# Retention followed by a four-expert MLP on one core: a batch's remainder on another queue, and the second token tile begun by halves between a later batch's units

## Chip, cores and metric

The kernel runs on one core of a Trainium2 chip. The metric is device time in microseconds for one execution, the median over the runs shown. The engines are named as in the profile: PE (TensorE matmuls), PEld (its weight loads), DVE (VectorE), ACT (ScalarE), POOL (GpSimd), SP (SyncE, which only issues DMAs here). POOL's DMAs go through a software queue, those of SP and ACT through hardware queues.

## The reference, cut to what matters

```python
# q, k, v: (B=8, H=8, S=576, D=64); moe_w1: (E=4, 512, F=1024); moe_w2: (4, 1024, 512)
scores = q @ k.T / 8                                  # per batch and head
Dmat = where(i >= j, gamma[h] ** (i - j), 0)          # decay with distance
x = ((scores * Dmat) @ v), heads side by side         # (4608, 512)
p = domain_probs / (sum over experts + 1e-9)          # (4608, 4)
out = sum over e of p[:, e] * (relu(x @ w1[e]) @ w2[e])
```

## The kernel before

**Two stages that overlap.** The tokens, 8 batches of 576, are cut into 9 tiles of 512 tokens (`t` = 0 to 8). A batch does not fill a tile evenly: tile 0 holds the first 512 tokens of batch 0, tile 1 the last 64 of batch 0 (its *remainder*) and 448 of batch 1, and so on. The retention stage writes the transposed tile `xt_of(t)` (bf16, features on the partitions); the MLP of tile `t` reads it. All work is put into one program order by hand; each engine runs its own instructions in that order and waits on semaphores for the others.

**Retention by units.** The first 512 tokens of batches 0 and 1 are done in four `Unit`s each: a unit is 256 tokens (`hf`) of four heads (`g`). A unit casts its raw k, q and v to bf16 with decay factors (`cast`, L526), transposes q and k either on PE (`trans_pe`, L534) or by DMA from SP (`trans_dma`, L547), multiplies scores and masks them on DVE (`scores`, L556), adds up the state `sbd` from k and v (`kv`, L587), and multiplies values (`values_own`, `values_carried`, L616 to L656), which ACT copies into `xt` (L649, L653). Batches 2 to 7 use a larger form, `Duo`. The remainder of each batch is a `Rem` (L320): loads (`load_rem`, L79: five DMAs, 384 KB in pieces of 256 bytes), casts, two DMA transposes on SP (L339), scores (L345), values (L351, L353).

**The MLP of a tile.** Up projections: 16 groups (`up_group`, L360), four per expert, each of 16 matmuls of 512 columns, followed on DVE by relu times the mixing weight `pB[t, e]` (L369) into `h`. Tile 0's first two groups are replaced by two `UpHalf`s (L374), each for 256 of the 512 tokens and four feature chunks, so that PE can begin before all tokens are there. Down projections: tile 0's first 256 tokens are done by plain products (`Plain`, L392, `po`), one block of eight matmuls per expert and half; its last 256 tokens, and all later tiles, by seven products per 256 tokens (`Down.product`, L448), which need sums of weights (`w_sum`, L410, tiles `t2w`, `t3w`, `t4w` and, in place, `wx[0]`) and sums of `h` (`sums`, L436), all on DVE.

**Loads.** POOL loads the weights, converted to bf16 on the way: `load_w1(e)` (L99, 1024 KB in the tile) and `load_w2(e)` (L102), and between them the mixing weights `pB` (`load_p`, L235). Line by line, L716 to L753 give POOL's order: pB of expert 1, w1 of expert 1, small tables, pB and w1 of experts 2 and 3, w2 of experts 0 and 1, batch 0's remainder, w2 of experts 2 and 3, then the raw tensors of batch 1's first two units (`load_v(0)`, `load_v(1)`). The raw tensors of batch 1's other two units are loaded from SP into the same buffers, after the first two have been cast (`v_cast`, L766).

**Slots.** What is neither an up group nor a product is hung on numbered slots: `add(i, f)` puts `f` into slot `i`, and `run(slots, n)` emits a slot's work after the n-th step of the tile. For tile 0, slots 0 to 15 follow the up groups (expert 0's first two are passed over, since the halves did them), 16 to 23 the plain products, 24 to 30 the seven products in the order 1, 5, 2, 3, 6, 7, 4 (L797 to L814). Batch 0's remainder stands at slots 17 (casts on DVE, transposes on SP), 20 (scores) and 21 (values); batch 1's units are at slots 23 to 29; `w_sum` at 20 to 27. From tile 1 on a slot table of 30 steps per tile is filled in the same way (L822 to L871).

**Buffers.** Accumulators in PSUM come from one ring of four (`ring_tile`); the accumulator `pd` of the seven products holds one of them until product 4 is read. `pB` and two of batch 1's bf16 buffers share a pool of four.

Of the kernel before, what the change touches and what calls it, by code (L numbers as in the profile page):

```python
# [23 lines left out]
def kernel(  # L24
# [10 lines left out]
    nc = tc.nc  # L35
    B, H, S, D = q.shape
    N, E = moe_domain_probs.shape
    _, Dm, F = moe_w1.shape
# [7 lines left out]
    NDC = Dm // 128  # L46
# [19 lines left out]
    def ring_tile(name, shape, dt=FP32):  # L66
        return ring.tile(shape, dt, tag="ring", name=name)
# [5 lines left out]
    def load_pair(t, b, p, eng=nc.sync):  # L73
        for n, src in srcs:
            for j in range(2):
                eng.dma_start(out=t[n][:, :, j, :],
                              in_=src[b, 2 * p + j, 0:SM, :].rearrange("(c p) d -> p c d", p=C))

    def load_rem(b, eng=nc.sync):  # L79
        for j in range(2):  # L80
            for n, src in (("k", k), ("v", v)):
                eng.dma_start(out=rawr[n][64 * j:64 * j + 64, :, j, :],
                                  in_=src[b, j:H:2, SM:S, :].rearrange("g t d -> t g d"))
        eng.dma_start(out=rawr["q"][0:R, :, :, :].rearrange("t g j d -> t (g j) d"),
                          in_=q[b, :, SM:S, :].rearrange("h t d -> t h d"))
# [3 lines left out]
    raw1 = {n: const.tile([128, NC, 2, D], FP32, name=f"raw1_{n}") for n, _ in srcs}  # L89
# [9 lines left out]
    def load_w1(e, f=slice(0, F)):  # L99
        return nc.gpsimd.dma_start(out=w1_sb[e][:, :, f], in_=moe_w1[e][:, f].rearrange("(dc p) f -> p dc f", p=128))  # L100

    def load_w2(e, lo=0, hi=NFC):  # L102
        c = (e % 2) * NFC
        return nc.gpsimd.dma_start(
            out=wx[e // 2][:, c + lo:c + hi, :, :].rearrange("p a b c -> p a (b c)"),
            in_=moe_w2[e][lo * 128:hi * 128, :].rearrange("(fc p) d -> p fc d", p=128))
# [67 lines left out]
    def later_tables():  # L174
        nc.gpsimd.memset(tri, 1.0)
        nc.gpsimd.affine_select(out=tri, in_=tri, compare_op=mybir.AluOpType.is_ge, fill=0.0,
                                base=0, channel_multiplier=-1, pattern=[[1, C]])
        nc.gpsimd.tensor_copy(trir[0:R], tri[0:R, 0:R])
        nc.gpsimd.tensor_copy(trir[R:2 * R], tri[R:2 * R, R:2 * R])
        nc.gpsimd.iota(pos_j[:, 0:NC], pattern=[[C, NC]], base=0, channel_multiplier=1,  # L180
                       allow_small_or_imprecise_dtypes=True)
        for j in range(2):
            nc.gpsimd.iota(pos_j[64 * j:64 * j + 64, NC:NC + 1], pattern=[[0, 1]], base=SM, channel_multiplier=1,
                           allow_small_or_imprecise_dtypes=True)
        for n in "kqv":
            nc.gpsimd.memset(rawr[n], 0.0)
# [46 lines left out]
    pB = {}  # L233

    def load_p(t, e, eng):  # L235
        pB[t, e] = ppool.tile([128, NT], FP32, tag="pB", name="pB")
        eng.dma_start(out=pB[t, e], in_=pd[e:e + 1, t * NT:(t + 1) * NT].to_broadcast([128, NT]))  # L237
# [4 lines left out]
    def xt_of(t):  # L242
        if t not in xt:
            xt[t] = xpool.tile([128, NDC, NT], BF16, tag="xt", name="xt")
        return xt[t]


    class Duo:
        def __init__(self, b, d):
            self.b, self.d = b, d  # L250
            self.ps = slice(2 * d, 2 * d + 2)
            self.qT, self.kT, self.sT = {}, {}, {}
# [107 lines left out]
    def up_group(h, t, e, i):  # L360
        ph = ring_tile("ph", [128, 2, NT])
        x = xt_of(t)
        for f in range(2):
            fc = 2 * i + f
            for dc in range(NDC):
                nc.tensor.matmul(ph[:, f, :], lhsT=w1_sb[e][:, dc, fc * 128:(fc + 1) * 128],  # L366
                                 rhs=x[:, dc, :], start=(dc == 0), stop=(dc == NDC - 1))
        fk = e * NFC + 2 * i
        nc.vector.scalar_tensor_tensor(h[:, fk:fk + 2, :], ph, 0.0,  # L369
                                       pB[t, e][:, :].unsqueeze(1).to_broadcast([128, 2, NT]), op0=MAX, op1=MULT)  # L370
        if i == NFC // 2 - 1 and 0 < t < n_nt - 1:
            load_p(t + 1, e, nc.gpsimd)

    class UpHalf:  # L374


        def __init__(self, half):
            self.c = slice(256 * half, 256 * half + 256)
            self.ph = ring_tile("ph", [128, 4, 256])

        def matmuls(self, i):
            for fc in range(2 * i, 2 * i + 2):
                for dc in range(NDC):
                    nc.tensor.matmul(self.ph[:, fc, :], lhsT=w1_sb[0][:, dc, fc * 128:(fc + 1) * 128],
                                     rhs=xt_of(0)[:, dc, self.c], start=(dc == 0), stop=(dc == NDC - 1))

        def relu(self, h):
            nc.vector.scalar_tensor_tensor(h[:, 0:4, self.c], self.ph, 0.0,
                                           pB[0, 0][:, self.c].unsqueeze(1).to_broadcast([128, 4, 256]),
                                           op0=MAX, op1=MULT)  # L390

    class Plain:  # L392
# [291 lines left out]
    for u in range(NU):  # L684
        if u + 2 < NU:
            cast_unit(u + 2)
        if u == NU - 1:
            part = UpHalf(0)
# [21 lines left out]
    h = hp.tile([128, E * NFC, NT], BF16, name="h")  # L710
    part.relu(h)
    part = UpHalf(1)
    part.matmuls(0)
    part.matmuls(1)
    part.relu(h)
    load_p(0, 1, nc.gpsimd)  # L716
    load_w1(1)
    later_tables()
    load_p(0, 2, nc.gpsimd)
    load_w1(2)  # L720
# [2 lines left out]
    load_w2(0, 0, NFC // 2)  # L723
    load_w2(0, NFC // 2, NFC)
    load_w2(1)
    load_rem(0, nc.gpsimd)
    load_w2(2)
    load_w2(3)
    down1 = Down(h, 0, 1)
# [25 lines left out]
    def run(slots, i):  # L755
        for f in slots.get(i, []):
            f()

    slots = {}
    add = lambda i, f: slots.setdefault(i, []).append(f)  # L760
    add(4, later_decays)
    rem0 = Rem(0)
    for at, f in ((17, lambda: rem0.cast(nc.vector)), (17, rem0.trans_dma), (20, rem0.scores), (21, rem0.values)):
        add(at, f)

    def v_cast(u):  # L766
        vs[u].cast("k", nc.gpsimd)
        vs[u].cast("q", nc.vector)
        vs[u].cast("v", nc.scalar if u < 0 else nc.gpsimd)
        if u > 1:  # L770
            vs[u].trans_dma()
        else:
            load_v(u + 2, nc.sync)

    def v_head(u):
        vs[u].scores()
        vs[u].kv()

    for u, (c, tr, sc, o) in enumerate(((23, 24, 25, 26), (24, 25, 26, 27), (25, 0, 27, 28), (26, 0, 28, 29))):
        add(c, lambda u=u: v_cast(u))  # L780
        if u < 2:
            add(tr, lambda u=u: vs[u].trans_pe())
        add(o, lambda u=u: vs[u].values())
        add(sc, lambda u=u: v_head(u))
    add(18, lambda: [load_p(1, e, nc.sync) for e in range(2)])
    add(30, lambda: [load_p(1, e, nc.sync) for e in range(2, E)])
    add(27, lambda: load_pair(raw1, 2, 0))
    add(27, lambda: load_rem(1))
    for which, ats in ((3, (20, 20, 21, 22)), (1, (21, 22, 23, 24)), (2, (24, 24, 25, 25)), (4, (26, 26, 27, 27))):
        for j, at in enumerate(ats):  # L790
# [20 lines left out]
    for m in (1, 5, 2, 3, 6, 7, 4):  # L811
        down1.product(m)
        run(slots, n)
        n += 1  # L814

    first.close()
    dpl = ctx.enter_context(tc.tile_pool(name="dpl", bufs=1))
# [5 lines left out]
    slots = {}  # L823
# [30 lines left out]
    for t in range(1, n_nt):  # L854
        d = [Down(h, t, s) for s in range(2)]
        for s in range(2):
            for i, which in enumerate((1, 2, 4, 3)):
                for lo in (0, KH // 2):
                    add(NS * (t - 1) + 16 + 7 * s + i - (3 if d[s].last and i == 0 else 0),
                        lambda s=s, which=which, lo=lo, d=d: d[s].sums(which, lo, lo + KH // 2))  # L860
        n = NS * (t - 1)
        for e in range(E):
            for i in range(4):
                up_group(h, t, e, i)
                run(slots, n)
                n += 1
        for s in range(2):
            for m in (1, 5, 2, 6, 3, 7, 4) if d[s].last else (1, 4, 2, 5, 6, 3, 7):
                d[s].product(m)
                run(slots, n)  # L870
                n += 1  # L871
# [30 lines left out]
```

## Time and profile before

| | us |
|---|---|
| Median of 12 runs | 548.55 |
| Lowest, highest | 545.28, 551.76 |
| The profiled execution | 546.64 |
| Its span (first to last instruction) | 544.4 |
| PE busy in the span | 527.5 |
| Mean granted TensorE clock | 0.994 |
| Tile 0's first up half (L384) begins | 18.0 |
| Plain products (L400) begin | 48.6 |
| Seven products (L469) begin | 72.2 |
| Tile 1's first up group begins | 94.3 |

The span is what the trace sees of the execution; the 2.2 us by which the execution is longer lie around it. All times of the trace count from the start of the span. A line of the timeline gives start, duration, engine, source line, operation, the tile written and the tiles read, and how often, then in brackets the idle time before it and what ended it. In a table of stretches each engine's busy time is followed by its number of instructions; then come the granted clock, the DMA share (the mean busy share of the 16 DMA engines, which can pass 1 where transfers overlap) and the GB/s.

### The profile page before, as it was taken

How to read it: one execution, taken by the hardware profiler on the slowest of the kernel's cores; microseconds unless marked ns; L12 is line 12 of the kernel's file. 1: busy time of each engine (PE TensorE's matmuls, PEld its weight loads, DVE VectorE, ACT ScalarE, POOL GpSimd, SP SyncE). 2: the span in 40 equal slices, each digit the busy share in tenths (PEclk: the TensorE clock that was granted, in tenths of full speed). 3: DMA queues.
4: the chain of work that ended last, by engine and by line, in shares of the span. 5: the costliest groups of instructions: out<-in, count | busy, mean ns of one | idle time of the engine just before them, and what ended most of it. 6: DMA issues, size and time to landing. Idle time of an engine off the chain costs nothing.

```text
span 544.4 us, 10332 instructions
## 1 busy us (share of the span) xinstructions
PE 527.5 (97%) x4299; PEld 347.4 (64%) x4299; DVE 380.2 (70%) x472; ACT 68.8 (13%) x156; POOL 154.0 (28%) x196
## 2 busy tenths in 40 slices
PE   7999598999999999999999999999999999999997
PEld 3644266448854787458755885588547844884486
DVE  7668497677667874777677777687776567556763
ACT  4300042010310221111011001110101000000000
POOL 5824140445334424316222452235000000000000
PEclk9999899999999999999999999999999999999999
DMA  8999956856767858555646483635101111010001
GB/s 236 205 221 210 240 163 126 189 126 155 172 145 174 171 140 187 101 122 145 152 96 117 108 172 85 147 73 134 54 19 40 40 59 39 20 59 20 0 21 58
DMA packets 149950, 64.53 MB, mean 119 GB/s; under 512 B 125168, under 2 KB 140912, under 8 KB 149904
## 3 DMA queue, kind: packets, MB, share of 16 engines
q1 hardware_dynamic: 138224, 45.19, 36.3%
q0 software_dynamic: 11008, 18.48, 16.2%
q8 instruction: 33, 0.54, 0.4%
q10 hardware_dynamic: 672, 0.20, 0.2%
q14 instruction: 13, 0.11, 0.1%
HBM read 54.35 MB, written 9.51 MB: 117 GB/s over the span
## 4 chain that ended last, share of the span: by engine, by line
PE 72%; ACT 2%; DVE 0%; issue 0%
PE ph L366 36%; PE pd L469 33%; ACT xt L309 2%; PE o L301 1%; PE o L296 1%; PE py L469 1%; DVE h L369 0%; PE s L286 0%; PE or L351 0%; PE sr L345 0%; PE or L353 0%; PE kvp L272 0%; DVE ob L502 0%
## 5 line engine op out<-in xcount | busy, mean ns | idle before, releaser
L366 PE MATMUL ph<-xt,w 128*128 128x512 bf16 x1136 | 250.0, 379 | 2.5 <-DMA w<-in_moe_w_dram 1.9
L369 DVE SCALAR_TENSOR_TENSOR h<-ph,pB 128x1024 bf16<-128x1024 f32 x142 | 173.7, 1224 | 69.7 <-PE ph L366 69.5
L366 PEld LDWEIGHTS <-w 128*128 128x128 bf16 x1136 | 110.2, 98 | 130.9 <-DMA w<-in_moe_w_dram 2.4
L469 PEld LDWEIGHTS <-h 128*128 128x128 bf16 x1088 | 106.1, 98 | 14.6 <-issue 0.2
L469 PEld LDWEIGHTS <-s 128*128 128x128 bf16 x816 | 79.5, 98 | 9.4
L469 PE MATMUL pd<-wx,h 128*128 128x256 bf16 x544 | 64.9, 273 | 0.2
L469 PE MATMUL pd<-wx,s 128*128 128x256 bf16 x544 | 65.0, 273 | 0.0
L237 POOL DMA_DIRECT2D pB<-pd x31 | 17.5, 565 | 153.8 <-DVE h L369 141.0
L511 POOL TENSOR_TENSOR ob<-v,p 128x256 f32<-128x256 f32 x16 | 12.5, 780 | 126.1 <-DVE v L509 91.7
L256 POOL TENSOR_TENSOR bf_k<-raw_k,gk 128x512 bf16<-128x512 f32 x24 | 26.1, 1087 | 35.5 <-DMA raw_k<-in_k_dram 14.9
L288 DVE TENSOR_TENSOR sT<-s,tri 128x1024 bf16<-128x1024 f32 x24 | 28.3, 1219 | 6.4 <-PE s L286 6.4
L442 DVE TENSOR_TENSOR s<-s,h 128x1024 bf16<-128x1024 bf16 x34 | 32.6, 999 | 0.0
L469 PE MATMUL pd<-t4w,h 128*128 128x256 bf16 x272 | 32.5, 273 | 0.0
L469 PE MATMUL pd<-t3w,h 128*128 128x256 bf16 x256 | 30.6, 273 | 0.3 <-DVE u L488 0.3
L469 PE MATMUL pd<-t2w,s 128*128 128x256 bf16 x256 | 30.6, 273 | 0.0
L256 POOL TENSOR_TENSOR bf_q<-raw_q,gq 128x512 bf16<-128x512 f32 x24 | 27.4, 1142 | 3.5 <-DMA raw_q<-in_q_dram 3.3
L309 ACT ACTIVATE xt<-o 128x768 bf16<-128x768 f32 (+6 forms) x24 | 13.1, 596 | 116.8 <-PE o L301 116.8
L446 DVE TENSOR_TENSOR s<-h,s 128x1024 bf16<-128x1024 bf16 x34 | 26.8, 829 | 0.0
L440 DVE TENSOR_TENSOR s<-h 128x1024 bf16<-128x1024 bf16 x34 | 25.6, 794 | 0.0
L477 ACT ACTIVATE p<-pd 128x256 f32<-128x256 f32 x17 | 6.6, 386 | 138.5 <-PE pd L469 112.7
L444 DVE TENSOR_TENSOR h<-h 128x1024 bf16<-128x1024 bf16 x34 | 22.6, 706 | 0.0
L488 DVE TENSOR_TENSOR u<-pd,p 128x256 f32<-128x256 f32 x16 | 6.8, 425 | 20.8 <-PE pd L469 20.7
(158 smaller groups left out, 347.0 us busy)
## 6 DMA issues: line engine op xcount, KB each, us to landing
pB<-pd POOLq DMA_DIRECT2D x31, 256.0 KB, 3.8
raw_k<-in_k_dram SPq DMA_DIRECT2D x48, 128.0 KB, 2.7
raw_q<-in_q_dram SPq DMA_DIRECT2D x48, 128.0 KB, 3.0
raw_v<-in_v_dram SPq DMA_DIRECT2D x48, 128.0 KB, 3.1
out_dram<-oa SPq DMA_DIRECT2D x19, 256.0 KB, 2.8
out_dram<-ob SPq DMA_DIRECT2D x16, 256.0 KB, 2.2
w<-in_moe_w_dram POOLq DMA_DIRECT2D x3, 1024.0 KB, 12.3
wx<-in_moe_w_dram POOLq DMA_DIRECT2D x3, 1024.0 KB, 20.0
```

The costliest lines, as they stand in the source:

```text
L237: eng.dma_start(out=pB[t, e], in_=pd[e:e + 1, t * NT:(t + 1) * NT].to_broadcast([128, NT]))
L256: eng.tensor_tensor(bfs[p % 2][n], raw1[n], g[:, :, 2 * p:2 * p + 2].unsqueeze(3).to_broadcast([128, NC, 2, D]), op=MULT)
L288: nc.vector.tensor_tensor(sT[:, :, :, :].rearrange("p j c t -> p (j c) t"), s[:, :, :, :].rearrange("p j c t -> p (j c) t"), tri[:, :].uns ...
L309: nc.scalar.activation(xt_of(t)[:, self.ps, n0 + a - t * NT:n0 + z - t * NT], o[:, :, a:z], Copy)
L366: nc.tensor.matmul(ph[:, f, :], lhsT=w1_sb[e][:, dc, fc * 128:(fc + 1) * 128], rhs=x[:, dc, :], start=(dc == 0), stop=(dc == NDC - 1))
L369: nc.vector.scalar_tensor_tensor(h[:, fk:fk + 2, :], ph, 0.0, pB[t, e][:, :].unsqueeze(1).to_broadcast([128, 2, NT]), op0=MAX, op1=MULT)
L440: nc.vector.tensor_tensor(self.alloc("s1")[:, l], h[:, l, self.b], h[:, r, self.b], op=ADD)
L442: nc.vector.tensor_tensor(self.alloc("s2")[:, l], self.s1[:, l], h[:, l, self.a], op=SUB)
L444: nc.vector.tensor_tensor(h[:, l, self.b], h[:, l, self.a], h[:, l, self.b], op=SUB)
L446: nc.vector.tensor_tensor(self.alloc("s4")[:, l], h[:, r, self.a], self.s2[:, l], op=SUB)
L469: mm = nc.tensor.matmul(dst, lhsT=src[:, kk, tok], rhs=rhs(c), start=(start and c == 0), stop=(c == KH - 1), skip_group_check=True)
L511: nc.gpsimd.tensor_tensor(self.ob[:, HF:Dm], self.v, self.p5, op=ADD)
```

## The change

Four things are moved. (1) w1 of expert 1 is loaded in two halves, the first ahead of the load of that expert's mixing weight on POOL's queue. (2) Batch 0's remainder is no longer loaded from POOL between w2 of experts 1 and 2, but from ACT at slot 5; its casts and transposes are at slot 13, its scores and values at slots 26 and 27. (3) Batch 1's units stand two to four slots later; the last two reach past the last product of tile 0. (4) The first two up groups of tile 1 become two halves of 256 tokens, between whose parts the last units stand. The load of batch 2's first pair moves from slot 27 to slot 29, so that batch 1's remainder, still at 27, is now issued before it and before the last units' transposes. In SP's program order after the change stand: two stores of `oa`, six raw loads of batch 1, the five loads of its remainder, a store of `oa`, the four transposes of units 2 and 3, the six loads of batch 2's first pair.

```diff
-        def __init__(self, half):
+        def __init__(self, half, t=0):
+            self.t = t
...
-                                     rhs=xt_of(0)[:, dc, self.c], start=(dc == 0), stop=(dc == NDC - 1))
+                                     rhs=xt_of(self.t)[:, dc, self.c], start=(dc == 0), stop=(dc == NDC - 1))
...
-                                           pB[0, 0][:, self.c].unsqueeze(1).to_broadcast([128, 4, 256]),
+                                           pB[self.t, 0][:, self.c].unsqueeze(1).to_broadcast([128, 4, 256]),
...
+    load_w1(1, slice(0, F // 2))
     load_p(0, 1, nc.gpsimd)
-    load_w1(1)
+    load_w1(1, slice(F // 2, F))
...
     load_w2(1)
-    load_rem(0, nc.gpsimd)
     load_w2(2)
...
-    for at, f in ((17, lambda: rem0.cast(nc.vector)), (17, rem0.trans_dma), (20, rem0.scores), (21, rem0.values)):
+    add(5, lambda: load_rem(0, nc.scalar))
+    for at, f in ((13, lambda: rem0.cast(nc.vector)), (13, rem0.trans_dma), (26, rem0.scores), (27, rem0.values)):
...
-    for u, (c, tr, sc, o) in enumerate(((23, 24, 25, 26), (24, 25, 26, 27), (25, 0, 27, 28), (26, 0, 28, 29))):
+    for u, (c, tr, sc, o) in enumerate(((25, 27, 28, 29), (26, 28, 29, 30), (28, 0, 30, "h1"), (29, 0, "h1", "h2"))):
...
-    add(27, lambda: load_pair(raw1, 2, 0))
+    add(29, lambda: load_pair(raw1, 2, 0))
...
         down1.product(m)
         run(slots, n)
         n += 1
+    for half in range(2):
+        part = UpHalf(half, 1)
+        part.matmuls(0)
+        if half == 0:
+            run(slots, "h1")
+        part.matmuls(1)
+        part.relu(h)
+        if half == 0:
+            run(slots, "h2")
...
-                up_group(h, t, e, i)
+                if t > 1 or e > 0 or i > 1:
+                    up_group(h, t, e, i)
```

In the unit table `c` is the slot of the casts, `tr` of the PE transposes, `sc` of scores and state, `o` of the values.

## The prediction

> **What bounds the kernel now.** I read the page, then who waited for whom on PE, then the PE and POOL timelines from 14 to 100 us, then the stretches of 1 and 2 us. TensorE is the bound:
>
> ```profile
> PE 527.5 (97%) x4299; PEld 347.4 (64%) x4299; DVE 380.2 (70%) x472; ACT 68.8 (13%) x156; POOL 154.0 (28%) x196
> ```
>
> PE waits little, and after 94 us hardly at all. So a change of order gains only what PE loses before that, and a time gained or lost there passes to the end one for one. The waits (total, times, longest):
>
> ```profile
> PE sr L345 <- DMA qTr<-bfr_q: 5.2, 1, 5.2
> PE ph L366 <- DMA w<-in_moe_w_dram: 1.9, 1, 1.9
> ...
> PE po L400 <- DMA wx<-in_moe_w_dram: 1.0, 1, 1.0
> PE s L565 <- DMA qkT<-q: 0.9, 1, 0.9
> ```
>
> The largest is the remainder's score product for the transposed q. The timeline shows where, and a second loss behind it:
>
> ```profile
> 48.63 7.07 PE L400 MATMUL po<-wx,h 128*128 128x512 bf16 x32
> 56.72 1.89 PE L400 MATMUL po<-wx,h 128*128 128x512 bf16 x8 [1.02 <-DMA wx<-in_moe_w_dram]
> 63.82 0.37 PE L345 MATMUL sr<-qTr,kTr 128*128 128x64 bf16 x4 [5.21 <-DMA qTr<-bfr_q]
> 64.00 3.60 PE L400 MATMUL po<-wx,h 128*128 128x512 bf16 x8
> ...
> 67.84 4.56 PE L400 MATMUL po<-wx,h 128*128 128x512 bf16 x16
> 72.24 1.91 PE L469 MATMUL pd<-wx,h 128*128 128x256 bf16 x16
> ```
>
> Eight products take 1.89 us at 56.72 and 3.60 us at 64.00. The stretches of 1 us give the reason in the clock column (after ACT and POOL): 0.50 from 63 to about 69.4. Until 69.4 PE ran 5.6 us at half speed and lost 2.8.
>
> ```profile
> 61.00:62.00 1.00, 0.00 (x0) 0.00 (x0) 0.00 (x0) 0.00 (x0) 0.00 (x0) 1.00 1.23 211
> 66.00:67.00 1.00, 1.00 (x4) 0.32 (x3) 1.00 (x2) 0.00 (x0) 0.73 (x1) 0.50 0.82 275
> 71.00:72.00 1.00, 1.00 (x6) 0.43 (x5) 1.00 (x2) 0.00 (x0) 0.73 (x1) 1.00 0.02 8
> ```
>
> So some 8 us hang on the remainder. But the DMA share (last but one) stands at 1.1 to 1.26 from 22 to 62 us: the engines are full with weights. POOL's issues show their pace, since each late one waits for the landing of the one eight before it in POOL's DMA order:
>
> ```profile
> 33.79 0.62 POOL L82 DMA_DIRECT2D rawr_k<-in_k_dram  x1 [4.08 <-DMA w<-in_moe_w_dram]
> 39.29 0.70 POOL L84 DMA_DIRECT2D rawr_q<-in_q_dram  x1 [4.27 <-DMA w<-in_moe_w_dram]
> 41.84 0.89 POOL L104 DMA_DIRECT2D wx<-in_moe_w_dram  x1 [1.85 <-DMA wx<-in_moe_w_dram]
> 45.06 0.89 POOL L104 DMA_DIRECT2D wx<-in_moe_w_dram  x1 [2.33 <-DMA wx<-in_moe_w_dram]
> 50.03 0.77 POOL L121 DMA_DIRECT2D raw_k<-in_k_dram  x1 [4.08 <-DMA wx<-in_moe_w_dram]
> ```
>
> Landings: w1 of expert 1 at 27.9, expert 2 at 33.6, expert 3 at 39.1; w2 of expert 1 at 49.9, some 5 us for each. The w2 tile's landing times are
>
> ```profile
> DMA to landing us min/median/max: 14.8/20.0/25.0
> ```
>
> 25.0 is expert 1 (issued 24.9), 14.8 expert 2 (41.84 + 14.8 = 56.6, when PE resumes); the page gives 20.0 as the median of the three whole loads, so it is expert 3: 45.06 + 20.0 = 65.1. **This is the number that decides.** The plain products of expert 3 (67.84 before) can't start before 65.1 in either kernel, unless the engines get less to do.
>
> **What the Trainium skill says.** "TensorE: Matmul & The Clock Gate", What's actually happening: an idle window of about 3.4 us, free-running, drops TensorE to half clock, and a busy one restores it. The trace agrees: half clock after 5.2 us idle, none after 1.9. "DMA: Bandwidth & Descriptors", Issuing engines are not separate DMA queues: DMAs of all issuers share the same 16 engines; only issue time is saved. The trace agrees: this qTr took 10.3 us to land among the weights, where the median is 3.6. "SBUF — State Buffer", SBUF: two separate sides: a GpSimd operation and a VectorE one with two SBUF inputs lock each other out. The trace agrees: L415 took 0.68 us alone, 1.53 beside POOL's casts.
>
> **The change, part by part.** (a) w1 of expert 1 in halves, the first ahead of pB. Its 2 MB landed at 27.9, some 5 us long, so the first half lands near 24.8, and PE asks at 26.0: the 1.9 us wait goes. The second half lands with pB near 27.9, needed at 29.5. The price is one more POOL issue, 0.75 us, on an idle POOL. What is late next is expert 2: 33.6, asked for at 33.0.
>
> (b) Batch 0's remainder leaves POOL's queue for ACT's, behind the decays (32.7 before, about 31 now). Five issues at 0.60 to 0.74 (SP's rows) are 3.3 us; ACT's next work is some 40 us later, so nobody waits. The bytes (384 KB, between 49.9 and 52.0 before: about 2.1 us) stay, only earlier: w1 of expert 2 may land at 33.6 to 35.7. Casts and transposes move from slot 17 to 13, so transposes and the two pB of tile 1 (also on SP) meet w2 of expert 1 rather than of experts 2 and 3. After 52.0 two w2 loads at 5.1 end at 62.2; at 65.1 they ended, so transposes and pB cost 2.9. All of it is still ahead of expert 3. The cost of the remainder's other queue is not in the trace: between -2.1 (it fits in gaps) and +1.5 us (256-byte pieces slow the weights more); I take 0: expert 3 at 65.1.
>
> (c) PE then runs at the DMAs' pace: up to 2.6 us at expert 2's up projections, then about 1.5 to 2 each at three w2 loads. That is the 1.9 and 5.2 back in small pieces, but each is under 3.4 us, so I take no half clock. Plain products end at 65.1 + 3.5 = 68.6, where before has 72.24: 3.6 gained.
>
> (d) Sums on DVE: L413/L415 now have no rem0 step ahead of them but still wait for 65.1; six of them, three beside POOL casts at up to 1.5, put the last L415 at 71.8. Product 5 needs it at 71.7: 0.1 to 0.9 lost; end 72.3.
>
> (e) Product 2, the remainder's scores (0.13), product 3, its values (0.42) and the first transposes end at 76.8; product 6 78.6; v0's scores and kv, v1's transposes 80.0; product 7 81.8; v0's values and v1's head 83.3; product 4 85.1; v1's values 85.6. All casts lie behind raw loads landing at 66 to 70, as before.
>
> (f) Now SP. Before v2's transposes stand: two stores of oa (71.2 to 72.8), six raw loads (0.4 to 0.5 each, q behind DVE's casts, to 77.3), the five remainder loads of batch 1 (3.3, formerly after the transposes, to 80.6), oa of product 6 (81.8). k goes at 81.9, q after its DVE cast at 83.1, landing 3.3 later (before: 81.67 to about 85): 86.4, asked for at 85.6. 0.8 lost. v2's scores and kv 87.4, half of half 0 (8 x 0.109) 88.3, v2's values wait for the sums into sbd (88.95), 0.5 lost; v3's q, 0.35 lost; second part 91.7; v3's values wait for sbd, 0.5; then half 1 needs ACT's copies of v3 (six, 0.93 us), where product 4 covered them before: 1.0 lost. Half 1 ends at 95.4.
>
> (g) Halves instead of groups: 32 x 0.109 = 3.5 against 16 x 0.217 = 3.5: nothing. The relu stays two operations. Slot 0 work of tile 1 follows at once; the batch 2 load stands behind v3's transposes on SP, landing near 94; its casts feed products at slot 13, some 19 us later: covered.
>
> **Sum.** Before, two up groups of tile 1 are done at 94.34 + 2 x 1.73 = 97.8; now at 95.4: 2.4 us less. The profiled run took 546.64 (span 544.4, 2.2 around it), so 544.2; it lies 1.9 below the median 548.55, which goes to 546.1, or 0.44% less. About 0.3% (1.6 us) is what a measurement of this kernel can tell from no change.
>
> **The rivals.** First, *the tail takes it back*: the four losses of (f) sum to 3.2 where before lost 2.0 (0.5, 0.3, 0.9, 0.3) at the same units. For it: nothing stands behind v1 to v3 but each other and 0.9 us pieces. If DVE or SP run 1.5 to 2 later than I worked out, 0.5 is left: 548.1. Second, *weights come sooner*: the remainder fits into gaps and expert 3 lands at 63: 2 more gained, 544.1. Against it: the DMA share has no gap from 28 to 62. Third, *one long wait*: the change spreads nothing, PE runs to expert 3 and stands there for 4 us; the half clock returns and costs 2.8: 548.9. Fourth, slower, *SP's order*: v2's transposed q lands after 89.0 rather than 86.4, through the remainder loads put ahead of it. Then PE idles 3.4 us, the clock halves over v2, v3 and the halves (about 3 us more), and 2.6 + 3.0 outweigh 2.4: 551.7. It decides where that wait passes one window. Against it: 2.6 us of slack in my chain.
>
> **How the numbers follow.** Forecast (1 to 4 gained) 0.50; sooner weights 0.11; tail 0.18; long wait 0.10; SP 0.11. Faster: 0.45 of the forecast's 0.50, the sooner weights and 0.02 of the tail: 0.58. Slower: SP, 0.04 of the long wait, 0.02 of the tail: 0.17. The rest, 0.25, is within 0.3%. The forecast's own range is 544.5 to 547.6; that for 8 in 10 goes from 543.4 (sooner weights with the lower price of (b)) to 549.5 (most of the long wait), leaving out SP's end.
>
> **What would show it.** Right: no wait at the first L366 of expert 1; no wait of L345 for qTr; several L400 waits for wx, the last ending near 65; clock 1.00 from 60 to 70; half 1 ending near 95; PE without gaps afterwards. Wrong: expert 3's weights far from 65, a clock of 0.50 anywhere after 20 us, or PE waiting over 2 us for qkT or xt between 80 and 95.

## The result, and the profile after the change

| | before | after |
|---|---|---|
| Median, us | 547.39 (49 runs) | 543.99 (12 runs) |
| Lowest, highest | 544.35, 551.76 | 542.73, 546.71 |
| The profiled execution | 546.64 | 542.33 |
| Its span | 544.4 | 540.6 |
| Mean granted clock in it | 0.994 | 0.997 |

The ratio is 0.9935, 95% interval 0.9914 to 0.9957: 0.65% faster, where 0.44% was forecast. The profiled executions differ by 3.8 us of span, where 2.4 was forecast. PE's work is nearly the same; the head of the page after:

```profile
PE 526.8 (97%) x4315; PEld 348.5 (64%) x4315; DVE 377.0 (70%) x472; ACT 68.7 (13%) x156; POOL 152.1 (28%) x192
```

Who PE waited for after the change (total, times, longest):

```profile
PE po L401 <- DMA wx<-in_moe_w_dram: 4.8, 2, 3.7
...
PE s L566 <- DMA qkT<-q: 1.3, 1, 1.3
...
PE ph L366 <- DMA w<-in_moe_w_dram: 0.4, 1, 0.4
```

The 5.2 us of L345 are gone, the 1.9 of L366 are 0.4, and the waits for w2 (`wx`) have grown from 1.0 to 4.8. The PE timeline of the same kernel shows where:

```profile
33.19 13.99 PE L366 MATMUL ph<-xt,w 128*128 128x512 bf16 x64 [0.35 <-DMA w<-in_moe_w_dram]
47.01 3.62 PE L401 MATMUL po<-wx,h 128*128 128x512 bf16 x16
51.77 3.61 PE L401 MATMUL po<-wx,h 128*128 128x512 bf16 x16 [1.14 <-DMA wx<-in_moe_w_dram]
59.05 8.75 PE L401 MATMUL po<-wx,h 128*128 128x512 bf16 x32 [3.66 <-DMA wx<-in_moe_w_dram]
67.64 1.91 PE L470 MATMUL pd<-wx,h 128*128 128x256 bf16 x16
...
85.90 0.42 PE L566 MATMUL s<-qkT 64*64 64x128 bf16 x16 [1.25 <-DMA qkT<-q]
...
92.07 1.99 PE L385 MATMUL ph<-xt,w 128*128 128x256 bf16 x14 [0.28 <-ACT xt L654]
93.89 6.42 PE L366 MATMUL ph<-xt,w 128*128 128x512 bf16 x29
```

PE runs at the pace of the weights: 1.14 us of waiting for expert 1, 3.66 for expert 2. The seven products begin at 67.64 (72.24 before), the two halves of tile 1 are done at 93.89 (97.8 before). The last 32 plain products took 8.75 us and not 7; the stretches of 1 us give the reason (after the name of the stretch and its length come PE, PEld, DVE, ACT, POOL, then the granted clock):

```profile
59.00:60.00 1.00, 0.95 (x5) 0.48 (x5) 0.90 (x2) 0.00 (x0) 0.00 (x0) 1.00 1.23 206
60.00:61.00 1.00, 1.00 (x5) 0.33 (x4) 0.39 (x1) 0.00 (x0) 0.00 (x0) 0.56 1.25 209
...
62.00:63.00 1.00, 1.00 (x4) 0.30 (x2) 0.00 (x0) 0.00 (x0) 0.00 (x0) 0.50 1.19 264
63.00:64.00 1.00, 1.00 (x5) 0.40 (x4) 0.00 (x0) 0.00 (x0) 0.00 (x0) 0.73 1.11 368
64.00:65.00 1.00, 1.00 (x6) 0.45 (x5) 0.80 (x2) 0.00 (x0) 0.00 (x0) 1.00 1.07 303
```

Half clock from about 60.1 to 63.5, which the prediction had ruled out. PE shows no wait for expert 3, but DVE, which needs the same weights for its sums, waited for them:

```profile
64.20 0.69 DVE L414 TENSOR_TENSOR t3w<-wx,wx 128x1024 bf16<-128x1024 bf16 x1 [3.81 <-DMA wx<-in_moe_w_dram]
```

Expert 3 landed just ahead of 64.2: the longest landing of the w2 tile, 35.4 us, after its issue at 28.67 gives 64.07. So the slow products of expert 2 ended when expert 3 came, and the half clock was spent on time that PE would otherwise have waited (e6 below tries this).

### The profile page after: what moved, and what is told of

Same layout as the page of the kernel before. It is cut to its first block, busy times and chain, and to the rows that moved or that the text cites. A ratio compares the mean times of both kernels' runs of the same rounds, so it can differ in the third digit from the quotient of the medians.

```text
span 540.6 us, 10375 instructions
## 1 busy us (share of the span) xinstructions
PE 526.8 (97%) x4315; PEld 348.5 (64%) x4315; DVE 377.0 (70%) x472; ACT 68.7 (13%) x156; POOL 152.1 (28%) x192
## 4 chain that ended last, share of the span: by engine, by line
PE 72%; ACT 2%; DVE 0%; issue 0%
PE ph L366 36%; PE pd L470 33%; ACT xt L309 2%; PE o L301 1%; PE o L296 1%; PE py L470 1%; DVE h L369 0%; PE or L351 0%; PE sr L345 0%; PE or L353 0%; DVE ob L503 0%
## 5 line engine op out<-in xcount | busy, mean ns | idle before, releaser
L366 PE MATMUL ph<-xt,w 128*128 128x512 bf16 x1120 | 246.6, 379 | 1.1 <-DMA w<-in_moe_w_dram 0.4
L369 DVE SCALAR_TENSOR_TENSOR h<-ph,pB 128x1024 bf16<-128x1024 f32 x140 | 171.1, 1224 | 65.2 <-PE ph L366 65.2
L366 PEld LDWEIGHTS <-w 128*128 128x128 bf16 x1120 | 108.6, 98 | 127.6 <-DMA w<-in_moe_w_dram 0.8
L512 POOL TENSOR_TENSOR ob<-v,p 128x256 f32<-128x256 f32 x16 | 12.0, 753 | 120.9 <-DVE v L510 95.5
L256 POOL TENSOR_TENSOR bf_k<-raw_k,gk 128x512 bf16<-128x512 f32 x24 | 26.3, 1094 | 37.2 <-DMA raw_k<-in_k_dram 13.0
L447 DVE TENSOR_TENSOR s<-h,s 128x1024 bf16<-128x1024 bf16 x34 | 26.8, 829 | 0.0
```

Of the source, the lines that this page charges most:

```text
L256: eng.tensor_tensor(bfs[p % 2][n], raw1[n], g[:, :, 2 * p:2 * p + 2].unsqueeze(3).to_broadcast([128, NC, 2, D]), op=MULT)
L447: nc.vector.tensor_tensor(self.alloc("s4")[:, l], h[:, r, self.a], self.s2[:, l], op=SUB)
L512: nc.gpsimd.tensor_tensor(self.ob[:, HF:Dm], self.v, self.p5, op=ADD)
```

## The experiments

Theory A, in all that follows: the landing of w2 sets when the plain products end; a wait that is taken away upstream comes back there; then the chain of batch 1's units (the *tail*) decides what is left. The rivals have letters as well, each with the numbers that it expects; for the wait of unit 2, F is that the buffer of the transposed q and k holds it up, G that SP's order does.

For the kernels before and after and for twelve runs the profiled execution gives these points. "Profiled" is its time. "Products": the seven products begin. "Done": two up groups of tile 1, or its two halves, are done (for kernels without halves: tile 1's beginning and twice 1.73). "Tail": the difference. "Rest": span less "done".

| | median (runs) | ratio to before, 95% | profiled | products | done | tail | rest |
|---|---|---|---|---|---|---|---|
| before | | | 546.64 | 72.24 | 97.8 | 25.6 | 446.6 |
| after | 543.99 (12) | 0.9935 (0.9914 to 0.9957) | 542.33 | 67.64 | 93.89 | 26.3 | 446.7 |
| e1 split only | 546.72 (22) | 0.9977 (0.9956 to 0.9998) | 544.29 | 68.91 | 95.8 | 26.9 | 446.5 |
| e2 no split | 544.57 (8) | 0.9915 (0.9881 to 0.9948) | 543.57 | 68.39 | 95.16 | 26.8 | 446.7 |
| e3 queue only | 544.92 (8) | 0.9923 (0.9892 to 0.9955) | 543.93 | 69.58 | 95.5 | 25.9 | 446.7 |
| e4 no halves | 546.48 (22) | 0.9967 (0.9948 to 0.9986) | 547.35 | 68.32 | 97.9 | 29.6 | 446.7 |
| e5 pB later | 542.41 (6) | 0.9895 (0.986 to 0.993) | 541.98 | 66.45 | 93.58 | 27.1 | 446.7 |
| e6 filler | 543.84 (6) | 0.9912 (0.9879 to 0.9945) | 543.89 | 69.29 | 95.47 | 26.2 | 446.7 |
| e7 own buffers | 543.89 (6) | 0.9907 (0.9878 to 0.9937) | 544.81 | 70.85 | 96.31 | 25.5 | 446.7 |
| e8 SP order | 546.3 (20) | 0.9972 (0.9951 to 0.9992) | 544.22 | 69.04 | 95.25 | 26.2 | 447.3 |
| e9 pB and buffers | 543.6 (6) | 0.9914 (0.988 to 0.9948) | 543.4 | 66.83 | 94.68 | 27.9 | 446.7 |
| e10 combined | 544.08 (8) | 0.9926 (0.9896 to 0.9956) | 542.53 | 66.99 | 93.97 | 27.0 | 446.5 |
| e11 queue and split | 545.28 (17) | 0.9945 (0.9927 to 0.9963) | 545.81 | 69.31 | 97.2 | 27.9 | 446.7 |
| e12 changed again | 543.35 (6) | 0.9901 (0.9866 to 0.9935) | 544.92 | 70.23 | 96.42 | 26.2 | 446.7 |

The rest is 446.6 within 0.1 in all but e8: what is won or lost before "done" reaches the end one for one. e1 to e4, e5 to e8 and e9 to e12 were each run on one chip beside runs of the kernel before (47, 25 and 24 of them). The points are of one execution each: those of after, e1, e5, e8 and e10 were the fastest of their kernels' runs, those of e7 and e12 the slowest. e12 is the changed kernel, and its weights landed 2.7 us later in its profile than in the first.

**e1, the split of w1 alone.** Base: before.

```diff
+    load_w1(1, slice(0, F // 2))
     load_p(0, 1, nc.gpsimd)
-    load_w1(1)
+    load_w1(1, slice(F // 2, F))
```

> The kernel before, with only w1 of expert 1 loaded in two halves, the first ahead of pB. Theory A (the weights' arrival paces PE until the last quarter of the plain products): the wait of 1.9 us at expert 1 goes, but the same time comes back at a later wait (w2 or the remainder's transposed q); ratio to before 0.999 to 1.001, expert 3's plain products begin at 67.5 to 68.2 as before. Rival B (each wait counts by itself): 1.9 us less, ratio 0.9965, the seven products begin near 70.3.

0.9977 lies between the two, and its interval holds both 0.9965 and 0.999: the medians do not decide. Where A named a place it missed. The PE timeline:

```profile
61.77 0.37 PE L345 MATMUL sr<-qTr,kTr 128*128 128x64 bf16 x4 [3.67 <-DMA qTr<-bfr_q]
...
65.46 3.62 PE L400 MATMUL po<-wx,h 128*128 128x512 bf16 x16
```

Expert 3's products begin at 65.46 and not at 67.5 to 68.2, the seven products at 68.91, sooner even than B's 70.3. qTr landed at 61.6 instead of 63.7, its wait fell to 3.7 us, and the half clock behind it lasted 3.4 us instead of 6.8; a second half clock in the tail, from 82.1 to 85.6, took part of this back (tail 26.9). But this was the fastest of 22 executions, 2.4 us under their median, so it shows what can happen in this kernel, not what usually does. What the split alone is worth stays open, between 0.1 and 2.4 us by the interval.

**e2, everything but the split.** Base: after, with the two lines of e1 undone.

> The changed kernel with w1 of expert 1 loaded whole again, behind pB. Theory A: the wait of some 1.9 us at expert 1 returns and the wait of 3.7 us for w2 of expert 2 shrinks to about 2; expert 3 begins near 64, ratio to before 0.9935 as the changed kernel's. Rival B: 1.9 us are lost, ratio 0.997.

The PE timeline:

```profile
28.03 22.58 PE L366 MATMUL ph<-xt,w 128*128 128x512 bf16 x94 [2.17 <-DMA w<-in_moe_w_dram]
50.45 7.07 PE L401 MATMUL po<-wx,h 128*128 128x512 bf16 x32
58.30 3.61 PE L401 MATMUL po<-wx,h 128*128 128x512 bf16 x15 [0.79 <-DMA wx<-in_moe_w_dram]
64.94 3.61 PE L401 MATMUL po<-wx,h 128*128 128x512 bf16 x16 [3.03 <-DMA wx<-in_moe_w_dram]
```

The wait at expert 1 is back (2.17), and a half clock follows it: the up projections from there on take 22.58 us, where they took 20.89 in the kernel before. By the clock column of the 1 us stretches it lasts from 28.92 to 32.32:

```profile
28.00:29.00 1.00, 0.97 (x5) 0.50 (x6) 0.00 (x0) 0.00 (x0) 0.73 (x1) 0.96 1.09 211
...
32.00:33.00 1.00, 1.00 (x6) 0.37 (x5) 1.00 (x17) 0.32 (x1) 0.00 (x0) 0.84 1.09 250
```

So some 3.9 us were lost early, and A still holds, for they come back as shorter waits later: there is no wait for expert 1's w2, expert 2's is short, and PE stands 3.03 us for expert 3, which lands at 64.94. Once the queue is changed, the split only moves a wait in this trace. 0.9915 has the changed kernel's 0.9935 in its interval and not B's 0.997.

**e3, the queue alone.** Base: before. The remainder's scores and values stay at slots 20 and 21.

```diff
-    load_rem(0, nc.gpsimd)
...
-    for at, f in ((17, lambda: rem0.cast(nc.vector)), (17, rem0.trans_dma), (20, rem0.scores), (21, rem0.values)):
+    add(5, lambda: load_rem(0, nc.scalar))
+    for at, f in ((13, lambda: rem0.cast(nc.vector)), (13, rem0.trans_dma), (20, rem0.scores), (21, rem0.values)):
```

> The kernel before, with only the remainder's load on ACT's queue at slot 5 and its casts and transposes at slot 13; its scores and values stay at slots 20 and 21, batch 1's units where they were, no halves in tile 1. Theory A: PE no longer waits for qTr, the plain products end at 67.6 to 68.5 instead of 72.2; but batch 1's units, whose raw tensors land no earlier, are now asked for 4 us sooner, and PE waits 2 to 4 us at them: ratio 0.996 to 0.999. Rival C (the queue is the whole of it, the rest is neutral): ratio 0.9935.

A miss: 0.9923, as good as the whole change within the intervals. I had expected 2 to 4 us of new waits at the units. The waits of PE:

```profile
PE po L400 <- DMA wx<-in_moe_w_dram: 3.6, 1, 3.6
PE ph L366 <- DMA w<-in_moe_w_dram: 2.0, 1, 2.0
...
PE s L565 <- DMA qkT<-q: 0.8, 1, 0.8
PE o L633 <- ACT sbd L608: 0.4, 2, 0.2
PE o L623 <- DVE sT L567: 0.4, 1, 0.4
PE pd L469 <- DVE u L488: 0.4, 1, 0.4
```

The units cost some 2 us, in pieces that the kernel before had too (its tail is 25.6, this one 25.9). Within the intervals the queue alone carries the gain.

**e4, without later units and halves.** Base: after; units, the pair's load and tile 1's up groups as before, the remainder's scores and values still at 26 and 27.

```diff
-    for u, (c, tr, sc, o) in enumerate(((25, 27, 28, 29), (26, 28, 29, 30), (28, 0, 30, "h1"), (29, 0, "h1", "h2"))):
+    for u, (c, tr, sc, o) in enumerate(((23, 24, 25, 26), (24, 25, 26, 27), (25, 0, 27, 28), (26, 0, 28, 29))):
...
-    add(29, lambda: load_pair(raw1, 2, 0))
+    add(27, lambda: load_pair(raw1, 2, 0))
...
```

> The changed kernel with batch 1's units back at their slots of before, batch 2's first load back at slot 27 and tile 1 begun by whole up groups; split, queue and slots of the remainder as changed. Theory A: as the run with the queue alone, within 0.5 us: 2 to 4 us of waits at the units, ratio 0.996 to 0.999. Rival C: as the changed kernel, 0.9935; then later units and halves are worth nothing.

The waits that are new in it:

```profile
PE kvp L580 <- DVE sTr L346: 2.0, 1, 2.0
PE pd L470 <- DVE wx L416: 1.4, 1, 1.4
```

With the remainder's scores at slot 26 among units at their old slots, PE waits 2.0 us for the remainder's mask on DVE and 1.4 for a weight sum, half clock follows from 80.3 to 83.7, and the tail is 29.6. A's number came, and C's 0.9935 lies outside the interval; but the kernel is 1.6 us slower than e3 on the same chip (0.7 to 2.5, from resampling the two medians), not within 0.5 of it. Later units and halves repair what slot 26 costs; how much else they give, e11 asks.

**e5, the mixing weights of tile 1 later.** Base: after.

```diff
-    add(18, lambda: [load_p(1, e, nc.sync) for e in range(2)])
+    add(24, lambda: [load_p(1, e, nc.sync) for e in range(2)])
```

> The changed kernel with the two pB loads of tile 1 moved on SP from slot 18 to slot 24, behind the stores of the plain products. Theory A (the 16 DMA engines set the pace up to expert 3's w2): 0.5 MB less stand ahead of it, w2 of experts 2 and 3 land about 1.2 us sooner (near 57.8 and 62.9), expert 3's products begin there, 1.0 to 1.3 us less than the changed kernel: ratio about 0.9915. Rival D (something else holds expert 3): no change, 0.9935, or 0.995 if the two loads now delay unit 2's raw tensors.

The PE timeline:

```profile
57.88 3.61 PE L401 MATMUL po<-wx,h 128*128 128x512 bf16 x15 [2.18 <-DMA wx<-in_moe_w_dram]
63.00 3.61 PE L401 MATMUL po<-wx,h 128*128 128x512 bf16 x16 [1.51 <-DMA wx<-in_moe_w_dram]
```

Two pB loads fewer stand ahead of the weights, and experts 2 and 3 land at 57.88 and 63.00. One profile would not show this, for two executions of the changed kernel differ by 2.7 us there. But in all three kernels with the later pB (e5, e9, e10) expert 3 lands between 63.0 and 63.5 and the products begin between 66.4 and 67.0; in the nine others with the remainder on ACT it is 64.1 to 66.7, and 67.6 to 70.9. That is the clearest support for A. In the median, 542.41, it is 1.4 us less than e6 on the same chip, which six runs each can't tell from nothing. And only 0.3 us of the 1.2 gained over the first profile are left at "done": the wait for unit 2's q has grown from 1.3 to 2.1.

**e6, a filler in the wait.** Base: after; 12 matmuls whose result nobody reads stand ahead of expert 2's products, so that PE is not idle there.

```diff
+            if e == 2 and g == 0:
+                w = ring_tile("w", [128, 512])
+                for _ in range(12):
+                    nc.tensor.matmul(w, lhsT=w1_sb[0][:, 0, 0:128], rhs=w1_sb[0][:, 0, 0:512], start=True, stop=True)
```

> The changed kernel with twelve matmuls of 512 columns, whose result nothing reads, ahead of expert 2's plain products, where PE waits 3.7 us and then runs at half clock. Theory A: the clock stays at 1.00 from 55 to 66, but expert 3's w2 still lands near 64: no gain, ratio 0.9935 within 0.0008. Rival E (the half clock after the wait costs what it seems to, 3.4 us at half speed): 1.7 us less, ratio 0.990.

The PE timeline:

```profile
60.74 3.61 PE L401 MATMUL po<-wx,h 128*128 128x512 bf16 x16 [0.75 <-DMA wx<-in_moe_w_dram]
65.84 3.61 PE L401 MATMUL po<-wx,h 128*128 128x512 bf16 x16 [1.49 <-DMA wx<-in_moe_w_dram]
```

The clock stays at 1.00, and the time comes back as 1.49 us of waiting for expert 3, as A says. In the changed kernel as in e6 the products begin some 3.5 us after expert 3's landing (64.07 and 65.8), so one stretch of half clock in this place is hidden. The ratios by themselves could not tell this, since the interval holds both forecasts. A second stretch is not hidden: in e7 two on end ran from 60.0 to 66.8, and the products began 4.7 us after the landing at 66.2.

**e7 and e8, why unit 2 waits for its q.** In the changed kernel SP shows a gap that its queue does not explain (an SP issue has its start and length ahead of its name):

```profile
78.67 0.62 SPq L84 DMA_DIRECT2D rawr_q<-in_q_dram  x1
79.40 0.55 SPq L492 DMA_DIRECT2D out_dram<-oa  x1
81.36 1.91 SPq L551 DMA_TRANSPOSE qkT<-kv  x1
83.36 1.21 SPq L551 DMA_TRANSPOSE qkT<-q  x1
```

SP is free at 79.95; the transpose of k goes at 81.36. `qkT` has two tiles, and unit 2 takes unit 0's, which PE reads last here (PE timeline of the same kernel), until 81.19:

```profile
80.91 0.28 PE L634 MATMUL o<-qkT,sbd 128*128 128x128 bf16 x2
```

e7 gives the transposed tiles of units 2 and 3 buffers of their own; e8 puts batch 1's remainder behind the transposes on SP. Base of both: after.

```diff
-            self.qk = atp.tile([128, 2, 2, 2, C], BF16, tag="qkT", name="qkT1")
+            self.qk = spool.tile([128, 2, 2, 2, C], BF16, tag="S", name="qkT1")
```

```diff
+    add(29, lambda: load_rem(1))
     add(29, lambda: load_pair(raw1, 2, 0))
-    add(27, lambda: load_rem(1))
```

> The changed kernel with the transposed q and k of units 2 and 3 in buffers of another pool (tag S), so that they needn't wait for the tiles of units 0 and 1. Theory F (unit 2's transposes wait for unit 0's tile, free at 81.2): they are issued from 80.0, PE's wait of 1.25 us for them goes, ratio 0.991 to 0.992. Rival G (the prediction: the loads ahead of them on SP hold them): no change, 0.9935.

> The changed kernel with the five remainder loads of batch 1 moved on SP behind the transposes of units 2 and 3. Theory F: SP is free 3.3 us sooner but the transposes still wait for unit 0's tile at 81.2: PE's wait of 1.25 us stays, ratio 0.9935. Rival G: the wait goes, ratio 0.991 to 0.992.

e7 on SP: no gap ahead of the transpose of k, and PE has no wait for `qkT` by DMA any more; its tail is the shortest of the kernels with halves, 25.5.

```profile
81.96 0.50 SPq L492 DMA_DIRECT2D out_dram<-oa  x1
82.57 1.23 SPq L551 DMA_TRANSPOSE qkT<-kv  x1
```

e8 on SP: free at 80.15 and still held until unit 0's last read (82.31 and 0.28); PE's wait for q is 1.1.

```profile
79.79 0.36 SPq L492 DMA_DIRECT2D out_dram<-oa  x1
82.76 1.21 SPq L551 DMA_TRANSPOSE qkT<-kv  x1
```

e7's products began 3.2 us later than the changed kernel's, which might have taken the wait away by itself. e12, the changed kernel with products as late (70.23), speaks against it: there SP is free at 82.28, k goes at 83.96, after unit 0's last read (83.79), and PE waits 1.15 us for q.

```profile
81.73 0.55 SPq L492 DMA_DIRECT2D out_dram<-oa  x1
83.96 1.79 SPq L551 DMA_TRANSPOSE qkT<-kv  x1
```

So the buffer held the transposes, not SP's order. In the medians this is not seen: 543.89 for e7, 543.84 for e6 on the same chip. e8's 0.9972 fits neither forecast: its interval leaves out 0.9935, and its median is 2.4 us above e7's on the same chip (1.3 to 3.5, by resampling). Its rest is 0.6 us longer, 0.4 of it a wait of the later remainder at tile 1's L345. Where the remaining 1.8 us come from, the profile, of the fastest of 20 executions, does not show; it stays open.

**e9 and e10, the combinations.** e9: e5 and e7 together. e10: e9, and batch 0's remainder back at slots 20 and 21, batch 1's loaded from POOL.

```diff
-    for at, f in ((13, lambda: rem0.cast(nc.vector)), (13, rem0.trans_dma), (26, rem0.scores), (27, rem0.values)):
+    for at, f in ((13, lambda: rem0.cast(nc.vector)), (13, rem0.trans_dma), (20, rem0.scores), (21, rem0.values)):
...
-    add(27, lambda: load_rem(1))
+    add(27, lambda: load_rem(1, nc.gpsimd))
```

> The changed kernel with the first mixing weights of tile 1 loaded at slot 24 rather than 18 (as in the run that loaded them late) and with tiles of their own for the DMA-transposed q and k of units 2 and 3. Theory A (weights set the plain products, then the two-tile buffer of the transposed q and k sets the tail): w2 of expert 3 lands at about 63, the wait for unit 2's q (2.1 us when only the mixing weights were moved) falls under 0.5, tile 1's second half ends near 91.5 to 92.5, ratio to the kernel before 0.985 to 0.988. Rival: the wait for q is set by the raw loads and casts ahead of the transposes, not by the buffer, once everything else is sooner: the wait stays over 1.5 us, the half ends at 93.5, ratio 0.9895 as with the mixing weights alone.

> As the run before it in this list, and besides batch 0's remainder has its scores and values at slots 20 and 21 again, ahead of w2 of the last experts, and batch 1's remainder is loaded from POOL's queue rather than SP's. Theory A: the 0.5 us of remainder products move into PE's waits for w2 and cost nothing there, SP is 3.3 us freer; the half of tile 1 ends 0.5 to 1 us earlier than in the run before, ratio 0.983 to 0.987. Rival: the remainder's masks on DVE at slot 20 delay the weight sums, product 5 or later waits by as much, and POOL's issues (5 at about 0.75 us) delay its casts: no better than the run before, 0.986 to 0.990.

Two misses. The products begin early (66.8 and 67.0), and the tail is longer by as much or more (27.9 and 27.0): unit 2 waits 1.5 and 2.3 us for q. In e9 SP has no gap left and the k transpose goes at 80.55, as in e5 (80.57): here it is SP's queue. In e10 SP is free of the remainder, but k goes at 79.70 and takes 5.5 us to land, with a DMA share of 1.55 from 80 to 84. In e9 the wait of 1.5 us also drew a half clock, this time on the path (stretches of 1 us, columns as above):

```profile
84.00:85.00 1.00, 0.00 (x0) 0.00 (x0) 0.19 (x1) 0.67 (x2) 1.00 (x2) 1.00 0.65 130
85.00:86.00 1.00, 0.63 (x20) 0.51 (x20) 0.17 (x1) 0.00 (x0) 1.00 (x2) 1.00 0.67 131
86.00:87.00 1.00, 1.00 (x10) 0.64 (x8) 1.00 (x2) 0.00 (x0) 0.19 (x1) 0.57 0.60 122
87.00:88.00 1.00, 1.00 (x6) 0.69 (x5) 0.81 (x3) 0.00 (x0) 0.00 (x0) 0.50 0.18 40
```

**e11, queue and split, and e12, the changed kernel again.** e11: e1 and e3 together, on the kernel before.

> The kernel before with the remainder's load on ACT's queue and w1 of expert 1 in halves; remainder's scores and values stay at slots 20 and 21, units at their old slots, no halves of tile 1. Theory B (the queue carries the gain; later units and halves only repair what the remainder's scores at slot 26 would cost): tile 1 begins at about 91.5 to 92, ratio 0.991 to 0.994, as the changed kernel. Rival A (units at the old slots cost 2 us of waits in the tail, halves are worth as much): ratio 0.995 to 0.997.

> The changed kernel once more, on the chip of the three others, for comparison with them. Ratio to the kernel before 0.9935 within 0.002; w2 of expert 3 lands between 63.5 and 65.5; if PE's wait for w2 of expert 2 passes 3.4 us, half clock follows for about one window, and otherwise not; unit 2's q wait 0.8 to 1.5 us. Nothing is to be told apart in it but how far executions of one kernel differ in where the weights land.

On one chip e11 took 545.28 and e12 543.35: 1.9 us less with later units and halves (0.9 to 2.6, from resampling the two medians). e11's 0.9945 lies between its two forecasts, and its interval reaches both. But the same step without the split, from e3 to e2 on another chip, brought 0.4 us (-0.7 to 1.9), so what later units and halves are worth beyond repairing slot 26 isn't settled: it was seen only beside the split. In e11's PE timeline a product of the tail takes 3.57 us instead of 1.9, after a wait of 1.23:

```profile
83.36 0.42 PE L565 MATMUL s<-qkT 64*64 64x128 bf16 x16 [1.23 <-DMA qkT<-q]
83.71 0.72 PE L579 MATMUL kvp<-kv 128*128 128x128 bf16 x8
84.37 3.57 PE L469 MATMUL pd<-t2w,s 128*128 128x256 bf16 x16
```

e12's ratio, 0.9901, is 0.0034 from the first one, more than the 0.002 expected. Its own profile had expert 3 at 66.7, later than the 63.5 to 65.5 expected. As expected, half clock followed the wait for expert 2, 3.48 us, from 60.90 to 64.32, and PE waited 1.15 us for q; the tail is 26.2 again (PE timeline):

```profile
61.68 4.90 PE L401 MATMUL po<-wx,h 128*128 128x512 bf16 x15 [3.48 <-DMA wx<-in_moe_w_dram]
66.78 3.61 PE L401 MATMUL po<-wx,h 128*128 128x512 bf16 x16 [0.20 <-DMA wx<-in_moe_w_dram]
```

No version beats the changed kernel beyond the intervals; e5 (542.41) was not run on one chip with it.

## Why the prediction was right, by its steps

The direction, the place and the main mechanism (the weights set the pace) were right; two steps were not, the clock in (c) and the losses in (f). The gain was about 3.4 to 3.8 us, and not 2.4. The median, 543.99, lies just below the forecast's own range (544.5 to 547.6) and inside that for 8 in 10. Of the 2.1 us between it and 546.1, 1.2 come from the kernel before, which 12 runs had put at 548.55 and 49 put at 547.39; the rest is the larger gain.

(a) Held: the wait at expert 1 is gone, expert 2's is 0.35. Once the queue is moved the split brings no gain that the runs can tell: e2 without it is as fast as the changed kernel, and e3 as e11, within the intervals.

(b), the number that decides, held: 65.1 forecast, 64.07 in the profile. In the kernels with the remainder on ACT it lay between 62.98 and some 66.8, and e5, e9 and e10 show that it moves with what is loaded ahead of it. With the same kernel it differed by 2.7 us (after and e12), so a single profile doesn't place it better than that, and that the forecast was only 1.0 off is partly luck.

(c) Right in that PE goes at the pace of the DMAs, wrong in "no half clock". The waits were not spread evenly; expert 2's was 3.66. The rule itself failed too: e2's wait of 2.17 us and e9's of 2.09 drew a drop. Here it cost nothing, because expert 3's weights were as late (e6). The price of the old half clock was read a little low: it lasted to 69.76, not 69.4 (0.62 in the stretch from 69 to 70), so PE lost 3.0 us in it rather than 2.8. The plain products end at 67.64 where 68.6 stood: 1.0 of the difference.

(d) Product 5 waited for nothing, where 0.1 to 0.9 was forecast.

(e) Held: from the products' start to unit 2's q the order and lengths are those worked out.

(f) The term that was mis-sized, and its reason was wrong. Forecast were 0.8 (v2's q), 0.5, 0.35, 0.5 and 1.0: 3.2. Measured were 1.25 for v2's q, none at v2's `sbd`, v3's q or v3's `sbd`, and 0.28 for ACT's copies: about 1.5. From the products to "done" 26.8 was forecast and 26.25 measured. v2's q was not late through SP's queue, which was free at 79.95 and not at 81.8, but through the two tiles of `qkT` (e7, e8, e12). I had followed SP's order and not asked what the next transpose may overwrite. Behind it a second error hid the first. From v2's q (86.4) to the end (95.4) the forecast had 9.0 us, 2.35 of them losses, so 6.65 of work; the trace has 8.0 (85.90 to 93.89), 0.3 of them losses, so 7.7. The losses were put 1.6 us too high and the work 1.05 too low, most of it in v3's values and half 1. That the two sums came out only 0.55 apart is luck.

(g) The halves' PE time is as forecast: 1.99 for 14 of the last 16. That fits an up group of 8 matmuls of 512 columns (1136 at L366 for 142 at L369), not the 16 of the description ahead. "Nothing" may have been too little for the pair of later units and halves: against e11 they gave 1.9 us, but from e3 to e2 no more than the noise.

Of the rivals, "weights come sooner" came closest in its number (544.1), but not with its mechanism: expert 3 landed at 64.07, not 63. "One long wait" happened, 3.66 us and half clock, without its price. "SP's order" lost: q landed at 85.9 and not after 89.0, and the buffer held the transposes.

**From profile to median.** The prediction carried the profile's difference to the median of before. The medians hold one thing more. Of the 96 runs of before that stood beside the experiments, 49 had a mean clock of 0.991 (median 547.6), 12 had 0.994 (546.65), 9 had 0.997 (545.99), 8 had 0.984 (551.16); the correlation of clock and time is -0.83. One stretch of 3.4 us at half clock takes 0.003 off the mean (0.5 x 3.4 / 545). The profile of before, at 0.994, had two; a mean of 0.991 points to three. Of 19 runs of the changed kernel 12 had 0.997, which points to one. A correlation is not a proof, and a stretch can be hidden (e6), but e2, e9 and e11 show one that slows PE's own work, so part of what the median gained is probably this.

**What stays open.** Why the tail grows when the products start earlier (e5, e9, e10). Buffer, SP's queue and the landing of transposes lie within about 1.5 us of each other, and each was last in one of the kernels; which would be last with all three relieved was not tried. Open too are what the split is worth on the old queue (e1), what later units and halves are worth without the split (e2, e3), and why most executions of e8 are slower than its profile.

## What to carry to other kernels

When a transfer sets the pace, move what is queued ahead of it first, and ask of every wait that you remove whether the same transfer is behind it: the split of w1 brought nothing that could be measured after the queue was moved. For a DMA into a rotating buffer, look for its issuer's gap and for the last reader of the tile that it overwrites, before blaming the queue's order. In a chain of small steps a wait of 1.2 us can cost another 1.7 through the clock: in e11 a product took 3.57 us instead of 1.9 behind one.

## What the runs showed of the hardware

The half clock comes in stretches of 3.41 us, or two on end (the kernel before, 62.94 to 69.76), and within an execution they start on a fixed grid. The starts are worked out from the granted clock of the 1 us stretches that they cut. In e9 they are 58.82 and 86.14, 8 x 3.415 apart; in e11 60.54 and 84.42, 7 x 3.411; in e1 61.66 and 82.14, in e4 59.86 and 80.34, both 6 x 3.413. The Trainium skill, "TensorE: Matmul & The Clock Gate", What's actually happening, gives a free-running window of 3413 ns, and the trace agrees. The same section lets the clock drop after an idle window, and there the trace differs: in the window of the grid just ahead of a drop PE was idle for 2.17 us (e2, drop at 28.92), 2.09 (e9, 58.82), 1.5 (e9, 86.14) and 1.4 (e11, 84.42), and not for all of it. The measurement decides.

The grid also explains a wait without a drop. In e2 the grid, ten windows after the drop at 28.92, has a boundary at 63.05, so the wait of 3.03 us, from 61.91 to 64.94, gives 1.14 us to one window and 1.89 to the next. That is less than the 2.17 that drew a drop in the same execution. The kernel before waited 1.87 us inside one window (25.39 to 28.80, counted back from 62.94) without a drop. In these traces, then, 1.89 us idle in a window of full matmuls left the clock alone and 2.09 did not, while in the tail 1.4 were enough. Perhaps the tail's small matmuls count for less; that was not tried. e10 waited 2.33 us in the tail without a drop, and with no drop anywhere its grid is not known.

Weights of the same kernel, with the same bytes ahead of them, landed up to 2.7 us apart from one execution to the next, after some 65 us. About half of that is there early: expert 2's up projections began at 33.19 in one and 34.53 in the other.
